# Every second attention head with V as the stationary operand, and VectorE's deferrable work emitted from one list

## The chip, the cores and the metric

The kernel runs on one core of a Trainium2 chip. Its time is the device time of that core in microseconds, the median of three runs. A profile of one further execution shows what each engine did: TensorE (PE, its weight loads apart as PEld), VectorE (DVE), ScalarE (ACT), GpSimd (POOL) and SyncE (SP), which here only starts transfers.

## What is computed

A layer norm of x (2048 tokens by 512), then two branches that are multiplied and added to x: attention over a cache of 2048 keys in 32 heads of 128, and a dense layer with a squared ReLU, through a SiLU. All tensors are bfloat16.

```python
xn = layernorm(x)                                    # 2048 x 512
q  = (xn @ wq).reshape(S, 32, 128)                   # per head
p  = softmax(q @ k_cache[h].T * 128**-0.5)           # 2048 x 2048 per head
s  = concat_h(p @ v_cache[h]) @ wo                   # 4096 -> 512
h  = relu(xn @ w1 + b1) ** 2                         # 512 -> 1792
g  = silu(h @ w2 + b2)                               # 1792 -> 512
out = x + s * g
```

## The kernel before

The kernel is one program in which every engine's instructions are laid out at build time, in order. It goes through 4 blocks of 512 queries x 32 heads = 128 "heads" g, each in 8 steps ("pairs" of key tiles): 1024 steps in all. In a step TensorE computes two score tiles (keys on the partitions, 512 queries along the row), ScalarE takes their exponential into one of 8 pT buffers, and TensorE multiplies pT of two steps ago with V. Between these lie the matmuls of the projections, of the dense branch and of the output projection, one or two per step, from a list of jobs; each job's result in one of two PSUM banks (psF) is taken out by VectorE.

The product of pT with V comes in two forms. In an ordinary head pT is the stationary operand, and V, with a column of ones for the softmax denominator, is streamed:

```python
# gen_pv: 8 matmuls of 129 columns in each of the 8 steps
t = E(PE, partial(_mm_shared, out=bankO(b)[:, qt % 2 * 256:qt % 2 * 256 + Dh + 1],
                  lhsT=pT[:, ps % NPT, p0:p0 + P],
                  rhs=v_sb[:, i, tt, 0:Dh + 1], ...))
# [...] at the end of the head: two copies out of PSUM, reciprocal, scaling, transposing DMA
```

In a V-stationary head V is the stationary operand and pT is streamed, so that the output comes transposed, as the output projection wants it, but without denominators. VectorE sums these from pT, and a trip through DRAM spreads them over the partitions:

```python
def is_b(g):
    return g % 4 == 1 and 4 < g < NG - 2           # 31 of the 128 heads

# gen_pv_b: 2 matmuls of 512 columns in each of the 8 steps
t_PV[pi] = E(PE, partial(_mm, out=bankO(0), lhsT=v_sb[:, i, tt, 0:Dh],
                         rhs=pT[:, pi % NPT, n * QB:(n + 1) * QB], ...))
# at the end of the head ScalarE copies the bank to o_b(g), a view of o_un

def den_part(pi):                                   # VectorE, once per step
    k = pi % NPR
    t_part[pi] = E(DV, partial(_reduce_t, out=d_part[:, k, :],
                               in_=pT[:, pi % NPT, :].rearrange("p (b j) -> p b j", j=32)),
                   deps=[t_exp[pi], t_den[0]])

def den_sum(g):                                     # d_sum, then DRAM and back
    t_den[0] = E(DV, partial(_reduce, out=d_sum[:], ...))
    t_den[1] = S.emit_dma(GP, partial(_dma, out=d_scr, in_=d_sum[:]), ...)
    for a in range(4):
        t_den[2] = S.emit_dma(GP, partial(_dma, out=d_quad[32 * a:32 * (a + 1), :, :], in_=src), ...)

def den_spread(g):                                  # d_rec: sum of 4, reciprocal; r_all: spread
    # [...]
def den_scale(g):                                   # oT = o_b(g) * r_all
    # [...]

def plan_b(g):                                      # fixed steps
    first = NPR * g + LAG
    for k in range(NPR):
        at_once.setdefault(first + 3 * k // 2, []).append(partial(den_part, NPR * g + k))
    at_once.setdefault(first + 12, []).append(partial(den_sum, g))
    at_once.setdefault(first + 19, []).append(partial(den_spread, g))
    at_once.setdefault(first + 20, []).append(partial(den_scale, g))
```

A pT buffer is written again 8 steps later, when both the matmuls and den_part have read it:

```python
t_exp[pi] = E(AC, partial(_act, out=pT[:, pi % NPT, :], in_=psA[...], func=ACT.Exp, ...),
              deps=[t, t_PV[pi - NPT] if pi >= NPT else None, t_part.get(pi - NPT)])
```

The two banks psO of an ordinary head are copied out by VectorE at its end (o_un); the next head's first product waits for the copy.

Of the kernel before, what the change touches and what calls it, by code (L numbers as in the profile page):

```python
# [227 lines left out]
def bass_recurrent_scan__mha_block_cached__dense_activation_squared_relu__prompt_kernel(  # L228
# [33 lines left out]
    LAG = 2  # L262
    VW = 136
# [7 lines left out]
    E = S.emit  # L271
# [16 lines left out]
    o_un = sb("o_un", [P, 2, TPB, Dh + 2], F32)  # L288
    rden = sb("rden", [P, 2, TPB], F32)
# [25 lines left out]
    tmp_t = sb("tmp_t", [P, 2, D], F32)  # L315
# [31 lines left out]

    def is_b(g):
        return g % 4 == 1 and 4 < g < NG - 2
# [207 lines left out]
    def gen_scores(pi):  # L557
        g, k = divmod(pi, NPR)
        s2, i = pi % 2, g % NSL
        assert t_kfill[g] is not None and t_evac[g] is not None  # L560
        t = None
        if g == 0:
            qt, b = divmod(pi, 2)
            for c in range(NKT // 2):
                t = E(PE, partial(_mm_shared, out=psA[:, s2 * 1024 + c * P:s2 * 1024 + (c + 1) * P],
                                  lhsT=kT[:, 0, (b * NKT // 2 + c) * P:(b * NKT // 2 + c + 1) * P],
                                  rhs=qt_sb[:, 0, qt * P:(qt + 1) * P], start=True, stop=True),
                      deps=[t_k0[b], t_q0[qt], t_exp[pi - 2] if pi >= 2 else t_b1[0]],
                      inc=(c == NKT // 2 - 1))
        else:  # L570
            for n in range(2):
                tt = 2 * k + n
                t = E(PE, partial(_mm, out=psA[:, s2 * 1024 + n * 512:s2 * 1024 + (n + 1) * 512],
                                  lhsT=kT[:, i, tt * P:(tt + 1) * P], rhs=qt_sb[:, g % NQS, :],
                                  start=True, stop=True),
                      deps=[t_exp[pi - 2] if pi >= 2 else None, t_kfill[g], t_evac[g],
                            t_bankF[0] if pi == 0 else None],
                      inc=(n == 1))
        if k == NPR - 1:
            t_S_last[g] = t  # L580
        t_exp[pi] = E(AC, partial(_act, out=pT[:, pi % NPT, :],
                                  in_=psA[:, s2 * 1024:(s2 + 1) * 1024],
                                  func=ACT.Exp, scale=SM_SCALE),
                      deps=[t, t_PV[pi - NPT] if pi >= NPT else None, t_part.get(pi - NPT)])
# [3 lines left out]
    t_obf = [None, None]  # L588
    t_part = {}
    t_den = [None] * 6  # L590
    later = []

    def gen_pv_b(pi):
        g, k = divmod(pi, NPR)
        i = g % NSL
        for n in range(2):
            tt = 2 * k + n
            t_PV[pi] = E(PE, partial(_mm, out=bankO(0), lhsT=v_sb[:, i, tt, 0:Dh],
                                     rhs=pT[:, pi % NPT, n * QB:(n + 1) * QB],
                                     start=(tt == 0), stop=(tt == NKT - 1)),  # L600
                         deps=[t_exp[pi], t_vfill[g], t_free[0]], inc=(n == 1))
        if k == NPR - 1:
            t_PV_last[g] = t_PV[pi]
            t_free[0] = E(AC, partial(_act, out=o_b(g), in_=bankO(0), func=ACT.Copy),
                          deps=[t_PV[pi], t_onorm[g - 2]])

    def o_b(g):
        return o_un[:, g % 2, :, :].rearrange("p t c -> p (t c)")[:, 0:QB]
# [7 lines left out]
    def den_sum(g):  # L616
        t_den[0] = E(DV, partial(_reduce, out=d_sum[:],
                                 in_=d_part[:].rearrange("p k (n b) -> p b (k n)", n=2)),
                     deps=[t_part[NPR * (g + 1) - 1], t_den[1]])
        t_den[1] = S.emit_dma(GP, partial(_dma, out=d_scr, in_=d_sum[:]), sl_dw,  # L620
                              deps=[t_den[0], t_den[2]])
        src = bass.AP(tensor=d_scr.tensor, offset=d_scr.offset,
                      ap=[[NBK, 32], [32 * NBK, 4], [1, NBK]])
        free = [t_den[1], t_den[3]]
        for a in range(4):
            t_den[2] = S.emit_dma(GP, partial(_dma, out=d_quad[32 * a:32 * (a + 1), :, :],
                                              in_=src), sl_dr, deps=free)

    def den_spread(g):
        t_den[3] = E(DV, partial(_reduce, out=d_rec[:],  # L630
                                 in_=d_quad[:].rearrange("p a b -> p b a")),
                     deps=[t_den[2], t_den[5]])
        t_den[4] = E(DV, partial(_recip, out=d_rec[:], in_=d_rec[:]), deps=[t_den[3]])
        base = d_rec[:]
# [5 lines left out]
    def den_scale(g):  # L640
        t_onorm[g] = tok_oT[g] = E(
# [3 lines left out]

    def plan_b(g):
        first = NPR * g + LAG
        for k in range(NPR):
            at_once.setdefault(first + 3 * k // 2, []).append(partial(den_part, NPR * g + k))
        at_once.setdefault(first + 12, []).append(partial(den_sum, g))  # L650
        at_once.setdefault(first + 19, []).append(partial(den_spread, g))
        at_once.setdefault(first + 20, []).append(partial(den_scale, g))

    def gen_pv(pi):
# [34 lines left out]
        if last:  # L689
            t_PV_last[g] = t  # L690
            s = g % 2
            for b in range(2):
# [3 lines left out]
                    deps=[t_bank[b], t_onorm[g - 2] if g >= 2 else None])  # L696
            tr = E(DV, partial(_recip, out=rden[:, s, :], in_=o_un[:, s, :, Dh]),
                   deps=[t_oev[g][0], t_oev[g][1], t_onorm[g - 2] if g >= 2 else None])
            base = rden[:, s, :]
            rb = bass.AP(tensor=base.tensor, offset=base.offset,  # L700
                         ap=[list(base.ap[0]), [1, TPB], [0, Dh]])
            t_onorm[g] = E(DV, partial(_tt, out=o_bf[:, s, :, :], in0=o_un[:, s, :, 0:Dh], in1=rb,
                                       op=ALU.mult),
                           deps=[tr, t_obf[s]])

    def gen_oT(g):
        if is_b(g):
            return
        tok_oT[g] = t_obf[g % 2] = S.emit_dma(
            SP, partial(_dmaT, out=oT[:, g % NOT, :].rearrange("p (t q) -> p t q", q=P),  # L710
                        in_=o_bf[:, g % 2, :, :].rearrange("p t d -> p (t d)")), sl_oT[g % 4],
# [5 lines left out]
    t_o2 = {}  # L717
    t_g = {}
    t_acc = {}
    t_u = {}  # L720
    t_outdma = [None, None]
# [6 lines left out]
    at_once = {}  # L728
# [27 lines left out]
    def job_h(j, c):  # L756
# [11 lines left out]
        def evac(bank, step):  # L768
            s = c % 2
            t1 = E(DV, partial(_ts, out=r_t[:, s, :], in0=bankF(bank), scalar1=b1f[:, c:c + 1],  # L770
                               scalar2=0.0, op0=ALU.add, op1=ALU.max),
                   deps=[box[0], t_b1[0], t_rt[s]])
            t_h2[j, c] = t_rt[s] = E(
                DV, partial(_tt, out=h2T[:, c, :], in0=r_t[:, s, :], in1=r_t[:, s, :],
                            op=ALU.mult),
                deps=[t1] + [t_o2[j - 1, qt] for qt in range(TPB) if j > 0])
# [3 lines left out]
    def job_o2(j, qt):  # L780
        jt = j * TPB + qt

        def mm(n, bank):
# [3 lines left out]
            if t is not None:  # L787
                t_o2[j, qt] = t

        def evac(bank, step):  # L790
            s = jt % 2
            tz = E(DV, partial(_tt, out=z_t[:, s, :], in0=bankF(bank), in1=b2bc[:], op=ALU.add),
                   deps=[t_o2[j, qt], tok_b2, t_zrd[s]])
# [13 lines left out]
            at(step + 3, gate)  # L807
# [5 lines left out]
    def job_wo(j, m, qt, c0=0, c1=D):  # L813
# [6 lines left out]
        def mm(n, bank):  # L820
            g = j * H + h0 + n
            place, free = (bankF(bank), t_bankF[bank]) if isinstance(bank, int) else bank
# [6 lines left out]
        def evac(bank, step):  # L829
# [11 lines left out]
            if m == len(CH[j]) - 2:  # L841
                at(step + 1, partial(pre_combine, j, qt))
            if last:
                s = jt % 2
                t = E(DV, partial(_stt, out=tmp_t[:, s, c0:c1], in0=place, scalar=0.5,
                                  in1=g_all[:, jt % (2 * TPB), c0:c1], op0=ALU.mult,
                                  op1=ALU.mult),
                      deps=[box[0], t_g[jt], t_tmp[s]])
# [21 lines left out]
    def pre_combine(j, qt):  # L870

        jt = j * TPB + qt
        if jt not in t_g:
            pending.append(partial(pre_combine, j, qt))
            return
        t = E(DV, partial(_stt, out=acc[:, qt, :], in0=acc[:, qt, :], scalar=0.5,
                          in1=g_all[:, jt % (2 * TPB), :], op0=ALU.mult, op1=ALU.mult),
              deps=[t_acc[qt], t_g[jt]])
        t_u[jt] = E(DV, partial(_tt, out=acc[:, qt, :], in0=acc[:, qt, :], in1=x_t[:, qt, :],
                                op=ALU.add), deps=[t, tok_xt[jt]])  # L880

# [4 lines left out]
    for j in range(NQB):  # L886
# [7 lines left out]
        for m, (h0, h1) in enumerate(CH[j]):  # L894
            if h1 == H and j == NQB - 1:
                continue
            for qt in range(TPB):
                r = j * SPB + NPR * h1 + (14 if h1 < H else 30)
                jobs.append((r + 30 + 15 * qt, r, job_wo(j, m, qt), None))
# [40 lines left out]
    def tail_one(step):  # L940
        i, x = tail_order[0]
        if step < NPAIR and step < NPR * ((NQB - 1) * H + CH[-1][-1][0] + x + 1) + 10:
            return False
# [60 lines left out]
    for j in range(NQB):  # L1004
        if j + 1 < NQB:
            for i in range(TPB):
                at(j * SPB + 3 * NPR, partial(ln_load, j + 1, i))
                at(j * SPB + 7 * NPR + 3 * i, partial(ln_stats, j + 1, i))
                at(j * SPB + 10 * NPR + 6 + NPR * i, partial(ln_next, j + 1, i))
# [65 lines left out]
    for pi in range(NPAIR):  # L1075
# [22 lines left out]
        for fn in at_once.pop(pi, []):  # L1098
            fn()
# [5 lines left out]
        if k == LAG + 1 and g >= 1:  # L1105
            gen_oT(g - 1)
        pending.extend(events.pop(pi, []))
        if k >= 2:
            for fn in [pending.pop(0) for _ in range(min(2, len(pending)))]:
                fn()  # L1110
    for pi in range(NPAIR - LAG, NPAIR):
        gen_pv(pi)
    gen_oT(NG - 1)
# [9 lines left out]
    assert not jobs and cur[0] is None and not events and not pending and not at_once  # L1123
# [32 lines left out]
```

## Time and profile before

| | |
|---|---|
| time, median of 3 runs | 1241.03 us (1239.99 to 1245.44) |
| span of the profiled execution | 1236.9 us |
| granted TensorE clock | 1.0 throughout |
| DMA, mean | 148 GB/s |

The page lists each engine's busy time, and groups of equal instructions as "out<-in" with their count, busy time and mean duration; behind it stands the idle time of the engine just before them and what ended it. Matmuls overlap, so their duration is longer than the distance from one start to the next. In the page's slices of the span ScalarE and VectorE look like this, in tenths of a fortieth:

```profile
DVE  4576655477766656546776666554686765556655
ACT  7888888888888888888888888888888888888894
```

The longest waits of the profile are VectorE's and GpSimd's, and are idle time of engines that have time to spare:

```profile
POOL d_scr L221 <- DVE d_sum L209: 892.8, 31, 60.0
DVE o_un L180 <- PE psO L158: 209.0, 85, 6.7
...
DVE d_rec L209 <- DMA d_quad<-d_scr: 46.4, 20, 6.0
```

The numbers behind the colon are microseconds in total, the number of waits, and the longest.

### The profile page before, as it was taken

To read this page: it belongs to the slowest core of one execution; us is meant where nothing else is said; L and a number is where in the kernel's file an instruction comes from. 1 tells how busy PE (TensorE), PEld (TensorE's weight loads), DVE (VectorE), ACT (ScalarE), POOL (GpSimd) and SP (SyncE) were. 2 spreads that over 40 slices of the span, in tenths; PEclk is the share of its full clock that TensorE was granted. 3 is DMA by queue.
4 is the path that set the end of the run, shared out by engine and by line. 5 is a ranking of instruction groups with operands and counts; after the bars stand their busy time and mean duration, and the time that the engine had idled before them with its cause. 6 is when DMAs were issued, how large, how long until landed. Compare 5 with 4: busy or idle time off the path is not lost.

```text
span 1236.9 us, 24563 instructions
## 1 busy us (share of the span) xinstructions
PE 1227.2 (99%) x10397; PEld 754.9 (61%) x10397; DVE 770.2 (62%) x1232; ACT 1062.6 (86%) x1075; POOL 117.7 (10%) x228
## 2 busy tenths in 40 slices
PE   9999999999999999999999999999999999999998
PEld 7665556655666655665555665556656556656565
DVE  4576655477766656546776666554686765556655
ACT  7888888888888888888888888888888888888894
POOL 1010100000012010000000201000000000100001
PEclk9999999999999999999999999999999999999999
DMA  9998987676788696877677878786777679787661
GB/s 219 213 222 168 192 193 130 135 139 132 137 156 153 121 173 137 147 141 131 130 132 170 149 133 159 141 150 130 136 146 135 139 151 147 147 142 143 133 121 28
DMA packets 674957, 182.47 MB, mean 148 GB/s; under 512 B 659152, under 2 KB 673664, under 8 KB 674848
## 3 DMA queue, kind: packets, MB, share of 16 engines
q1 hardware_dynamic: 667792, 175.55, 75.1%
q0 software_dynamic: 6384, 5.09, 2.3%
q8 instruction: 82, 1.34, 0.5%
q10 hardware_dynamic: 672, 0.26, 0.1%
q14 instruction: 27, 0.22, 0.1%
HBM read 97.62 MB, written 2.35 MB: 81 GB/s over the span
## 4 chain that ended last, share of the span: by engine, by line
PE 88%; DVE 6%; DMA 4%; issue 1%; POOL 1%; SPq 0%; DVEq 0%
PE psA L153 32%; PE psO L158 25%; PE psF L153 23%; PE psO L153 8%; DVE d_part L213 2%; DMA d_quad<-d_scr 2%; DMA d_scr<-d_sum 1%; POOL d_quad L221 1%; DVE qt_sb L180 0%; DVE r_t L172 0%; DVE acc L166 0%; DMA kT<-in_A_k_cache_dram 0%; DVE o_un L180 0%; DVE oT L166 0%; DVE h2T L166 0%
## 5 line engine op out<-in xcount | busy, mean ns | idle before, releaser
L162 ACT ACTIVATE pT<-psA 128x1024 bf16<-128x1024 f32 x1024 | 1040.9, 1024 | 153.9 <-PE psA L153 115.3
L153 PE MATMUL psA<-qt_sb,kT 128*128 128x512 bf16 x2032 | 604.3, 379 | 0.0
L158 PEld LDWEIGHTS psO<-v_sb,pT 128*128 128x128 bf16 x6208 | 414.7, 98 | 186.5 <-issue 13.1
L158 PE MATMUL psO<-v_sb,pT 128*128 128x129 bf16 x6208 | 478.2, 220 | 3.8 <-DVE o_un L180 3.8
L213 DVE TRANSPOSE_TENSOR_REDUCE d_part<-pT 128x32 f32<-128x1024 bf16 x248 | 291.9, 1217 | 0.0
L180 DVE COPY o_un<-psO 128x258 f32<-128x258 f32 x194 | 73.8, 421 | 209.6 <-PE psO L158 209.0
L153 PEld LDWEIGHTS psA<-qt_sb,kT 128*128 128x128 bf16 x2032 | 167.1, 98 | 58.6
L153 PE MATMUL psF<-xnT,wq_sb 128*128 128x512 bf16 (+1 forms) x520 | 168.7, 374 | 0.1
L153 PE MATMUL psF<-wo_all,oT 128*128 128x512 bf16 x480 | 163.7, 379 | 1.6 <-DVE oT L166 1.6
L153 PE MATMUL psO<-pT,v_sb 128*128 128x512 bf16 x496 | 147.5, 379 | 0.0
L180 DVE CAST qt_sb<-psF 128x512 bf16<-128x512 f32 (+1 forms) x130 | 86.6, 666 | 56.1 <-PE psF L153 55.7
L221 POOL DMA_DIRECT2D d_scr<-d_sum x31 | 17.4, 562 | 892.8 <-DVE d_sum L209 892.8
L153 PEld LDWEIGHTS psF<-xnT,wq_sb 128*128 128x128 bf16 x520 | 50.3, 98 | 59.8 <-DVE xnT L180 0.2
L153 PEld LDWEIGHTS psO<-pT,v_sb 128*128 128x128 bf16 x496 | 48.5, 98 | 58.6 <-issue 2.8
L153 PEld LDWEIGHTS psF<-wo_all,oT 128*128 128x128 bf16 x480 | 46.9, 98 | 58.3 <-DVE oT L166 2.1
L153 PE MATMUL psF<-xnT,w_sb 128*128 128x512 bf16 x224 | 77.1, 379 | 0.0
L153 PE MATMUL psF<-w_sb,h2T 128*128 128x512 bf16 x224 | 74.1, 379 | 0.0
L221 POOL DMA_DIRECT2D d_quad<-d_scr x124 | 67.6, 552 | 68.1 <-DMA d_scr<-d_sum 64.8
L166 DVE TENSOR_TENSOR o_bf<-o_un,rden 128x512 bf16<-128x512 f32 x97 | 67.1, 692 | 3.8 <-DVE rden L184 0.5
L172 DVE TENSOR_SCALAR r_t<-psF,b1f 128x512 bf16<-128x512 f32 x56 | 41.2, 736 | 45.2 <-PE psF L153 45.2
L153 PEld LDWEIGHTS psF<-w_sb,h2T 128*128 128x128 bf16 x224 | 21.9, 98 | 26.4
L153 PEld LDWEIGHTS psF<-xnT,w_sb 128*128 128x128 bf16 x224 | 21.9, 98 | 26.4
(58 smaller groups left out, 338.8 us busy)
## 6 DMA issues: line engine op xcount, KB each, us to landing
v_sb<-in_A_v_cache_dram SPq DMA_DIRECT2D x127, 512.0 KB, 4.6
wq_sb<-in_A_wq_dram SPq DMA_DIRECT2D x127, 128.0 KB, 3.3
wo_all<-in_A_wo_dram SPq DMA_DIRECT2D x4, 1024.0 KB, 6.1
w_sb<-in_B_w_dram SPq DMA_DIRECT2D x14, 256.0 KB, 4.3
x_t<-in_A_x_dram POOLq DMA_DIRECT2D x16, 128.0 KB, 3.4
kT<-in_A_k_cache_dram SPq DMA_TRANSPOSE x127, 4.4
d_quad<-d_scr POOLq DMA_DIRECT2D x124, 8.0 KB, 3.5
x_ln<-in_A_x_dram SPq DMA_DIRECT2D x15, 128.0 KB, 3.8
```

The lines of the kernel that those rows point to most:

```text
L153: return e.matmul(out, lhsT, rhs, start=start, stop=stop)
L158: return e.matmul(out, lhsT, rhs, start=start, stop=stop, skip_group_check=True)
L162: return e.activation(out, in_, func, bias=bias, scale=scale)
L166: return e.tensor_tensor(out, in0, in1, op)
L172: return e.tensor_scalar(out, in0, scalar1=scalar1, scalar2=scalar2, op0=op0, op1=op1)
L180: return e.tensor_copy(out, in_)
L213: return e.tensor_reduce(out, in_, axis=AX.X, op=ALU.add, apply_transpose=True)
L221: return e.dma_start(out, in_)
```

## The change

Three things. First, V is stationary in every second head from 4 to 124, 61 instead of 31. Second, VectorE's work that nobody waits for at once (the denominators' parts and their end, the normalising of ordinary heads, the squaring in the dense branch, gating, layer norm of the next block) is no longer put at fixed steps but into one list, each entry with the first step at which it may be emitted and the step at which it must. At build time an account is kept of how far TensorE and VectorE have come; a piece is emitted when VectorE is no more than ROOM = 1000 ns ahead of TensorE in this account (250 ns in the first step of a head), or when it is due. Third, V-stationary heads get output buffers of their own (o_col), and the buffers of the ordinary heads are counted by ordinary heads alone, so that each kind alternates between two; room for it comes from letting tmp_t be z_t.

```diff
+    clock = {"PE": 0.0, "DVE": 0.0}
+    def E(eng, fn, deps=(), inc=True):
+        if eng is PE:
+            clock["PE"] += free_size(fn.keywords["out"]) / 2.4 + 2.5
+        elif eng is DV:
+            n = max(free_size(fn.keywords[k]) for k in ("out", "in_") if k in fn.keywords)
+            clock["DVE"] = max(clock["DVE"], clock["PE"]) + n / 0.96 + 75
+        return S.emit(eng, fn, deps=deps, inc=inc)
[...]
+    o_col = sb("o_col", [P, 2, QB], F32)
-    tmp_t = sb("tmp_t", [P, 2, D], F32)
+    tmp_t = z_t
[...]
+    b_heads = [g for g in range(4, NG - 3, 2)]
     def is_b(g):
-        return g % 4 == 1 and 4 < g < NG - 2
+        return g in b_no
[...]
     def plan_b(g):
-        first = NPR * g + LAG
+        first = NPR * g
         for k in range(NPR):
-            at_once.setdefault(first + 3 * k // 2, []).append(partial(den_part, NPR * g + k))
-        at_once.setdefault(first + 12, []).append(partial(den_sum, g))
-        at_once.setdefault(first + 19, []).append(partial(den_spread, g))
-        at_once.setdefault(first + 20, []).append(partial(den_scale, g))
+            calm(first + k + 1, first + k + NPT - 2, partial(den_part, NPR * g + k))
+        calm(first + NPR, first + NPR + 8, partial(den_sum, g))
+    def fill_quiet(step, room, flush=False):
+        while quiet:
+            some = [x for x in quiet if may_run(x, step, flush)]
+            some = [x for x in some if x is not fresh[0]] or some
+            if not some:
+                break
+            x = min(some, key=lambda x: x[1])
+            if not flush and step < x[1] and clock["DVE"] - clock["PE"] > room:
+                break
+            fn = x[2].pop(0)
+            fn()
+            fresh[0] = x
+            if not x[2]:
+                quiet.remove(x)
+            if fn.func is den_sum:
+                g = fn.args[0]
+                calm(step + 10, step + 16, partial(den_total, g), partial(den_recip, g),
+                     partial(den_spread, g), partial(den_scale, g))
[...]
             for b in range(2):                        # end of an ordinary head
                 t_free[b] = t_oev[g][b] = E(DV, partial(_copy, out=o_un[...], in_=bankO(b)...), ...)
-            tr = E(DV, partial(_recip, ...))
-            t_onorm[g] = E(DV, partial(_tt, out=o_bf[:, s, :, :], ...))
+            calm(pi + LAG, pi + LAG + 3, partial(norm_recip, g), partial(norm_scale, g))
[...]
-            t_h2[j, c] = t_rt[s] = E(DV, partial(_tt, out=h2T[:, c, :], ...))
+            calm(step, step + 3, square)
-            at(step + 3, gate)
+            calm(step + 3, step + 8, gate)
-                at(step + 1, partial(pre_combine, j, qt))
+                calm(step + 1, step + 16, partial(acc_gate, j, qt), partial(acc_add, j, qt))
[...]
-                r = j * SPB + NPR * h1 + (14 if h1 < H else 30)
-                jobs.append((r + 30 + 15 * qt, r, job_wo(j, m, qt), None))
+                r = j * SPB + NPR * h1 + (24 if h1 < H else 30)
+                jobs.append((r + 20 + 15 * qt, r, job_wo(j, m, qt), None))
[...]
-                at(j * SPB + 7 * NPR + 3 * i, partial(ln_stats, j + 1, i))
-                at(j * SPB + 10 * NPR + 6 + NPR * i, partial(ln_next, j + 1, i))
+                b = j * SPB + 8 * NPR + 4 * NPR * i
+                calm(b, b + 24, partial(ln_bn, j + 1, i), partial(ln_rstd, j + 1, i))
+                calm(b + 28, b + 48, partial(ln_scale, j + 1, i), partial(ln_transpose, j + 1, i))
[...]
-        for fn in at_once.pop(pi, []):
-            fn()
+        fill_quiet(pi, 250 if k == 0 else ROOM)
```

The output projection of a group of heads is released 10 steps later, as a V-stationary head's output may now come later; its deadline stays. The matmuls of the last group are let in 26 steps after a V-stationary head's end instead of 10.

## The prediction

> **What bounds the kernel now.** I read four views in this order: the page's engine line, the costliest groups, the waits, and two stretches of the timeline.
>
> The engine line and two groups of the page:
>
> ```profile
> span 1236.9 us, 24563 instructions
> PE 1227.2 (99%) x10397; PEld 754.9 (61%) x10397; DVE 770.2 (62%) x1232; ACT 1062.6 (86%) x1075; POOL 117.7 (10%) x228
> ...
> L158 PE MATMUL psO<-v_sb,pT 128*128 128x129 bf16 x6208 | 478.2, 220 | 3.8 <-DVE o_un L180 3.8
> L213 DVE TRANSPOSE_TENSOR_REDUCE d_part<-pT 128x32 f32<-128x1024 bf16 x248 | 291.9, 1217 | 0.0
> ...
> L153 PE MATMUL psO<-pT,v_sb 128*128 128x512 bf16 x496 | 147.5, 379 | 0.0
> ```
>
> TensorE is busy for 99% of the span, VectorE for 62%, ScalarE for 86%. The mean of a matmul (220 or 379 ns) is its latency, not its price: matmuls overlap, so the price has to come from starts. The chain of waits gives it:
>
> ```profile
> 1221.64 1.36 PE psO L158 x24
> 1223.00 3.45 PE psF L153 x16
> ```
>
> A 129-column matmul takes 1.36/24 = 0.0567 us of TensorE, a 512-column one 3.45/16 = 0.2156 us. That these two prices explain the whole span shows that TensorE is the bound: 6208 x 0.0567 = 352 us, and (2032 + 504 + 480 + 496 + 224 + 224 + 16, all 512 wide by their groups) 3976 x 0.2156 = 857 us, together 1209 us. The small matmuls of start and end add about 15 us. What is left, some 12 us, is the wait for the first data, the drain at the end and stalls.
>
> How much of it is stall is in the waits of TensorE:
>
> ```profile
> PE psO L158 <- DVE o_un L180: 3.8, 5, 1.5
> PE psF L153 <- DVE oT L166: 1.6, 1, 1.6
> ```
>
> Six stalls, 5.4 us. As a matmul's shown end lies 0.16 us behind the next one's start, each is 0.16 us longer than shown: 6.4 us. The timeline shows how one comes about, VectorE first and TensorE below it:
>
> ```profile
> 273.62 0.26 DVE L209 TENSOR_REDUCE d_rec<-d_quad 128x16 f32<-128x64 f32 x1 [3.33 <-DMA d_quad<-d_scr]
> ...
> 276.73 0.68 DVE L166 TENSOR_TENSOR oT<-o_un,r_all 128x512 bf16<-128x512 f32 x1
> 277.51 0.76 DVE L180 COPY o_un<-psO 128x258 f32<-128x258 f32 x2
> ```
> ```profile
> 276.43 0.38 PE L153 MATMUL psF<-wo_all,oT 128*128 128x512 bf16 x1
> 278.09 0.53 PE L158 MATMUL psO<-v_sb,pT 128*128 128x129 bf16 x6 [1.28 <-DVE o_un L180]
> ```
>
> VectorE stood 3.33 us in front of d_rec until the softmax denominators came back from DRAM. Behind it in the queue stood gating, a projection cast, the scaling, and only then the copy that frees the output bank. TensorE needed that bank at 276.65 and had it at 278.09.
>
> [...]the copy above waits behind a DMA that it doesn't need, and 98 ns of weight load per matmul don't show in a pitch of 56.7 ns. [...]six transpose-reductions in 6.79 us, 1.13 us each for 1024 elements[...].
>
> **The change part by part.**
>
> *30 more heads with V stationary (31 to 61).* An ordinary head has 64 matmuls of 129 columns, 64 x 0.0567 = 3.63 us; a V-stationary one has 16 of 512, 16 x 0.2156 = 3.45 us. That is 0.18 us a head, and x 30 it is 5.3 us, on the engine that sets the end. The gain comes only from the ones column (one in 129) and the fixed share per matmul: the product itself is as large as before.
>
> *What VectorE pays.* Such a head needs 8 transpose-reductions (8 x 1.13 = 9.04), d_sum 0.58, d_rec 0.26 + 0.25, r_all 0.71 and oT 0.69: 11.5 us. It saves two output copies (0.84), a reciprocal (0.18) and o_bf (0.69): 1.7 us. Net 9.8 us, x 30 = 295 us. VectorE goes from 770 to about 1065 us, 86% of a span near 1230. This is off the path as long as its order is right.
>
> *Where it is tightest.* A pair of heads takes 2 x 1236.9/128 = 19.3 us now. VectorE needs 11.5 + 1.7 for it, and a share of the rest: 770.2 - 31 x 11.5 - 97 x 1.7 = 249 us over 64 pairs, 3.9 us. Sum 17.1, 89%. Following the new order of instructions from one d_sum to the next in a stretch with the output projection (3 copies or adds of partial sums, 2 gatings, 2 casts, beside the two heads' own), the mean durations add to some 18.7 us; neighbours overlap by about 0.08 us (1.217 against 1.13), so some 17 us of 19.1. I find no stretch whose work is above TensorE's, so no stall is forced by quantity. Moments are left.
>
> *The deferred list.* It takes nothing away from VectorE; it moves the d_part, normalising, squaring, gating and layer-norm instructions so that they are emitted when VectorE is less than 1.0 us ahead of TensorE by the account, 0.25 us at a head's first step, just before the bank copies. The account's costs (1024/0.96 + 75 = 1142 ns for a d_part, 608 for 512 elements) are near the trace's pitch of 1130. And d_rec is now emitted at least 10 steps after d_sum, 10 x 1.2 = 12 us, where it was 7 steps, 8.4 us. The trip in the chain takes 3.38 (write) + about 0.3 + 1.62 (issue) + 3.85 (read) = 9.2 us. So the kind of wait shown above should nearly vanish. Of the 6.4 us of stalls I count 5 as removed, the one before the tail (oT of head 125) among them, as the last V-stationary head is now 124.
>
> *The rest.* ScalarE: 30 more copies of an output bank x 0.592 = 18 us, to 1080 us, still below 90%. GpSimd: 5 issues x 0.55 us x 30 = 83 us, at 16% nobody waits for it. 30 transposing DMAs of oT fall away. The separate o_col buffers let V-stationary outputs wait for scaling without holding the ordinary heads' copies. The z_t buffer now serves tmp_t as well, which ties the gating to the final combination; with few of them in a stage it should cost nothing.
>
> *Sum.* -5.3 - 5 + new stalls. For these I take 4 us: about one in four of the 60 changes to a V-stationary head meets a d_part of 1.13 us just begun and loses about 0.25 us. Net -6.3, 1241.0 to 1234.7; rounded to 1234.
>
> **The rivals.**
>
> *A: VectorE becomes the bound in moments.* It holds 1.1-us instructions, with 2 us to spare in two heads, and a late d_part holds its pT buffer, then the exponential eight pairs on, then TensorE. For it: the load near 90%, and the account that puts tiny instructions at 75 to 80 ns where d_sum alone takes 580. Against it: exponentials have about 0.2 us per pair in hand (1.02 against 1.2) and scores run two pairs ahead. It would cost 5 to 20 us and make 1236 to 1250.
>
> *B: The DRAM trip comes late more often.* 61 trips, one every 19 us; the longest read in the chain took 5.12 us, 1.3 more than usual, and d_sum itself can run a microsecond or two after its emission. If one trip in four blocks VectorE as at 273 us, at 1.4 us each, that is 21 us: 1250. Against it: of the 20 times VectorE waited for this DMA (46 us) only a few reached TensorE, even with 3.6 us less room.
>
> *C: All old stalls vanish and no new ones come.* 1241.0 - 5.3 - 6.4 = 1229.3. For it speaks that the account is fitted to the trace's pitch; against it, that 60 changes of head must then all go well.
>
> **Range and chances.** C is the floor, as nothing else on TensorE is removed; a mild form of A makes the upper end. 1229 to 1242 should hold it 8 times in 10. Over 2% faster would be under 1216, below the floor: 0.01. Over 2% slower, above 1266, needs A and B together or a dependence that I overlook: 0.03. Within 2%: 0.96.
>
> **What would show it right or wrong.** Right: 67 x 64 = 4288 matmuls psO<-v_sb,pT instead of 6208 and 61 x 16 = 976 psO<-pT,v_sb instead of 496, TensorE still at 99%, VectorE at 86%, idle time before d_rec below 46 us in spite of twice as many, TensorE's waits for o_un and oT at a few us in all. Wrong: waits of TensorE for o_un, of ScalarE for d_part, or of psF matmuls for a cast, adding up to more than 10 us; or VectorE idle in front of d_rec as before. A pitch other than 0.0567 and 0.2156 us[...] would break the first term.

## The result, and the profile after

The changed kernel takes 1229.63 us (median of 4 runs, 1229.31 to 1231.01) against 1241.48 us for the kernel before in the same comparison: a ratio of 0.9902, 95% interval 0.9877 to 0.9926. That is 1.0% less, inside the predicted range and at its fast end.

The page of the changed kernel, the engine line and the groups that answer to those shown before:

```profile
span 1229.2 us, 22035 instructions
PE 1213.5 (99%) x8793; PEld 694.7 (57%) x8957; DVE 1028.9 (84%) x1502; ACT 1071.3 (87%) x1105; POOL 200.5 (16%) x378
...
L213 DVE TRANSPOSE_TENSOR_REDUCE d_part<-pT 128x32 f32<-128x1024 bf16 x488 | 575.4, 1216 | 0.0
...
L158 PE MATMUL psO<-v_sb,pT 128*128 128x129 bf16 x4288 | 330.2, 220 | 0.8 <-ACT pT L162 0.3
L153 PE MATMUL psO<-pT,v_sb 128*128 128x512 bf16 x957 | 286.2, 379 | 0.8
```

VectorE works 259 us more (a d_part takes 1216 ns on the mean, 1217 before) and TensorE is still busy throughout. 164 matmul records are missing in this trace (8793 matmuls, 8957 weight loads), which is why 957 stand where 976 ran; a gap of one matmul's length in it is no stall. The pitch has not changed. In the chain of waits of this kernel:

```profile
1190.13 0.68 PE psO L158 x12
...
1216.83 1.29 PE psA L153 x6
```

0.68/12 = 0.0567 us and 1.29/6 = 0.215 us, as before.

What changed most is the list of waits. These are VectorE's in front of d_rec and all three of TensorE's:

```profile
DVE d_rec L209 <- DMA d_quad<-d_scr: 2.7, 1, 2.7
...
PE psA L153 <- POOL mhalf L188: 1.0, 1, 1.0
PE psO L197 <- DMA kT<-in_A_k_cache_dram: 0.7, 1, 0.7
PE psO L158 <- ACT pT L162: 0.3, 1, 0.3
```

The first two of TensorE's lie in the first 6 us, the last behind the last exponential; in between the view lists none. Both waits shown before (for o_un and for oT) are gone, and VectorE stands in front of d_rec for 2.7 us instead of 46.4, with twice as many trips.

To see where the time went, I cut each trace at two instructions that all versions share, the start of the 9th and of the last exponential. Most experiments are read in these stretches too.

| us | up to 9th exponential | 9th to last (1015 steps) | last to end | span |
|---|---|---|---|---|
| before | 17.06 | 1202.65 | 17.17 | 1236.9 |
| after | 18.70 | 1192.53 | 17.98 | 1229.2 |
| 31 heads with the list (experiment 1) | 17.18 | 1197.73 | 16.02 | 1230.9 |

The middle gained 10.1 us. The first stretch lasted 1.6 us longer in this one execution. Some 0.9 us of it is the first K tile, which came later (its first use starts at 5.72 us instead of 4.79); in nearly the same program, experiment 3, the stretch took 17.03. This execution (1231.01 us) is also the slowest of the four, so the median carries little of it. The end, which should have gained too, lost 0.8 us.

### The profile page after: what moved, and what is told of

Same layout as the page of the kernel before. It is cut to its first block, busy times and chain, and to the rows that moved or that the text cites. A ratio compares the mean times of both kernels' runs of the same rounds, so it can differ in the third digit from the quotient of the medians.

```text
span 1229.2 us, 22035 instructions
## 1 busy us (share of the span) xinstructions
PE 1213.5 (99%) x8793; PEld 694.7 (57%) x8957; DVE 1028.9 (84%) x1502; ACT 1071.3 (87%) x1105; POOL 200.5 (16%) x378
## 3 DMA queue, kind: packets, MB, share of 16 engines
q0 software_dynamic: 11184, 6.32, 3.0%
## 4 chain that ended last, share of the span: by engine, by line
PE 98%; issue 1%; DMA 0%; ACT 0%; DVE 0%; ACTq 0%; SPq 0%; DVEq 0%
PE psA L153 35%; PE psF L153 25%; PE psO L158 20%; PE psO L153 17%; DMA kT<-in_A_k_cache_dram 0%; ACT pT L162 0%; PE psA L158 0%; PE psO L197 0%; PE psF L197 0%; DVE out_t L166 0%; DVE z_t L176 0%; ACTq L135 0%; DVE xnT L180 0%; SPq L221 0%; PE psA L197 0%
## 5 line engine op out<-in xcount | busy, mean ns | idle before, releaser
L153 PE MATMUL psA<-qt_sb,kT 128*128 128x512 bf16 x1909 | 577.8, 379 | 5.8
L213 DVE TRANSPOSE_TENSOR_REDUCE d_part<-pT 128x32 f32<-128x1024 bf16 x488 | 575.4, 1216 | 0.0
L158 PEld LDWEIGHTS psO<-v_sb,pT 128*128 128x128 bf16 x4288 | 286.6, 98 | 125.2 <-ACT pT L162 0.6
L158 PE MATMUL psO<-v_sb,pT 128*128 128x129 bf16 x4288 | 330.2, 220 | 0.8 <-ACT pT L162 0.3
L153 PE MATMUL psO<-pT,v_sb 128*128 128x512 bf16 x957 | 286.2, 379 | 0.8
L153 PEld LDWEIGHTS psO<-pT,v_sb 128*128 128x128 bf16 x976 | 95.4, 98 | 115.2 <-issue 5.8
L221 POOL DMA_DIRECT2D d_quad<-d_scr x244 | 132.9, 551 | 144.6 <-DMA d_scr<-d_sum 139.3
L180 DVE COPY o_un<-psO 128x258 f32<-128x258 f32 x134 | 51.0, 422 | 124.2 <-PE psO L158 123.7
L166 DVE TENSOR_TENSOR oT<-o_col,r_all 128x512 bf16<-128x512 f32 x61 | 41.9, 687 | 2.6
L217 DVE STREAM_TRANSPOSE r_all<-d_rec 128x512 f32<-128x512 f32 x61 | 43.1, 707 | 1.2
```

Source lines behind the costliest of these rows:

```text
L153: return e.matmul(out, lhsT, rhs, start=start, stop=stop)
L158: return e.matmul(out, lhsT, rhs, start=start, stop=stop, skip_group_check=True)
L166: return e.tensor_tensor(out, in0, in1, op)
L180: return e.tensor_copy(out, in_)
L213: return e.tensor_reduce(out, in_, axis=AX.X, op=ALU.add, apply_transpose=True)
L217: return e.transpose(out, in_)
```

## The experiments

Theory: two separate gains, cheaper products in 30 more heads and fewer stalls through the order of VectorE's work. Rivals: only one of the two counts; or VectorE is at its edge; or only one feature of the new order (the later reading of the denominators, the buffers, the gate at a head's start) does it all.

### 1. The list with 31 heads

```diff
-    b_heads = [g for g in range(4, NG - 3, 2)]
+    b_heads = [g for g in range(4, NG - 3, 4)]
```

> The changed kernel with only 31 V-stationary heads (every fourth, 4 to 124) and all else as it is. Theory (two separate sources: wider matmuls 5.3 us, stalls removed by the list about 5 us): 1229.6 + 30 x 0.177 = 1234.9 us, 1233.5 to 1236.5, with TensorE's waits under 2 us. Rival 'the list alone' (the wider matmuls bring nothing that lasts): 1229 to 1231. Rival 'the wider matmuls alone': near the kernel before, 1239 to 1242.

Measured: 1232.79 us (1232.71 to 1232.88), ratio to before 0.9926 (0.9914 to 0.9939). Both sources exist, but the time missed my window. In the middle stretch the list (with its buffers and the later reading of the denominators) gives 1202.65 - 1197.73 = 4.92 us, and the 30 heads another 1197.73 - 1192.53 = 5.20, or 0.173 us a head, as worked out. The 2.0 us that the sum then lacks are in the last column: 16.02 us with 31 heads, 17.98 with 61.

### 2. 61 heads with the fixed steps

```diff
-        return g % 4 == 1 and 4 < g < NG - 2
+        return g % 2 == 0 and 3 < g < NG - 3
```

(and the last group's matmuls let in 18 steps after a V-stationary head's end instead of 10; the change takes 26.)

> The kernel before, with its fixed steps, and 61 V-stationary heads (every second, 4 to 124). Theory: 5.3 us less matmul time, but twice as many trips that VectorE waits for in front of work that TensorE needs, so stalls of 12 to 25 us in place of 6: 1241.5 - 5.3 + 6 to 19 = 1242 to 1255 us. Rival 'the wider matmuls alone': 1229 to 1236, as VectorE's 84% leaves room in any order. VectorE's idle time in front of d_rec: 70 us or more by the theory.

Measured: 1302.21 us (ratio 1.0493, 1.0473 to 1.0513). I had the direction and not the size: it is 60 us above the kernel before in the same comparison (1241.93). The waits of this kernel, TensorE's first:

```profile
PE psA L153 <- ACT pT L162: 14.1, 32, 1.2
PE psF L153 <- DVE r_t L172: 9.9, 10, 2.3
PE psF L153 <- DVE z_t L166: 9.8, 6, 3.2
PE psO L158 <- ACT o_un L162: 7.4, 9, 2.0
```
```profile
DVE d_rec L209 <- DMA d_quad<-d_scr: 111.6, 55, 5.4
...
ACT pT L162 <- DVE d_part L213: 37.9, 53, 2.2
```

VectorE loses 112 us in front of d_rec at a load of 81%; what it then does late holds up everybody: exponentials that wait for a pT buffer, psF banks, and the output bank through ScalarE's copy into the shared o_un.

### 3 and 4. No gate at the head's start; no account at all

```diff
-        fill_quiet(pi, 250 if k == 0 else ROOM)
+        fill_quiet(pi, ROOM)      # experiment 3
+        fill_quiet(pi, 1e9)       # experiment 4
```

> The changed kernel with the lead of 1000 ns allowed at every step, also at a head's first one (250 ns there in the change). Theory (the order at the change of heads matters): a d_part of 1.13 us stands in front of the bank copies o_un more often, TensorE waits for o_un 2 to 10 us in all: 1231 to 1239. Rival (the slack of a head is enough by itself): 1229 to 1231, waits for o_un under 1 us.

Measured: 1229.96 us (ratio 0.9905, 0.9890 to 0.9921), the middle stretch 1192.88 against 1192.53. No wait of TensorE for o_un at all. The gate is worth nothing that can be seen; the rival holds.

> The changed kernel without the account: each piece is emitted in the first step in which it is allowed, soonest deadline first. Theory (the account is what keeps VectorE's queue short in front of bank copies): d_part pieces come in bunches behind the d_rec chain and TensorE waits 8 to 40 us for o_un and psF banks: 1237 to 1270. Rival (later reading of the DRAM trip is all that counted): 1229 to 1232.

Measured: 1341.02 us (ratio 1.0812, 1.0789 to 1.0835), beyond my window. The same work, in another order. Of TensorE's waits 80.7 us are for results to be taken out of psF, these two groups the longest; for o_un it waits once, 0.3 us, so that half of the theory was wrong:

```profile
PE psF L153 <- DVE r_t L172: 24.4, 25, 3.6
PE psF L153 <- DVE acc L166: 21.6, 16, 2.6
```

Its timeline, VectorE first, then TensorE:

```profile
305.54 0.76 DVE L180 COPY o_un<-psO 128x258 f32<-128x258 f32 x2 [4.35 <-PE psO L158]
...
315.98 4.60 DVE L213 TRANSPOSE_TENSOR_REDUCE d_part<-pT 128x32 f32<-128x1024 bf16 x4
320.62 0.58 DVE L209 TENSOR_REDUCE d_sum<-d_part 128x16 f32<-128x256 f32 x1
321.11 0.69 DVE L166 TENSOR_TENSOR acc<-psF,acc 128x512 f32<-128x512 f32 x1
```
```profile
321.86 0.39 PE L153 MATMUL psF<-wo_all,oT 128*128 128x512 bf16 x1 [1.36 <-DVE acc L166]
```

VectorE idles 4.35 us before a head's end, has four d_part pieces and a d_sum in a row ten microseconds later, and TensorE's bank is emptied behind them. Here deadlines alone were not enough; the work had to be spread.

### 5. A lead of 3000 ns

```diff
-        fill_quiet(pi, 250 if k == 0 else ROOM)
+        fill_quiet(pi, 3000)
```

> The changed kernel with VectorE allowed to be 3000 ns ahead of TensorE in the account at every step (1000 in e3: 1230 us; without limit in e4: 1341 us). Theory: a psF bank is filled about every 3.4 us and must be empty by the time of the job after next, so a lead of 3 us plus the copy is just too much: 1235 to 1270 us, waits of TensorE for psF results. Rival (only a lead without limit hurts): 1229 to 1232.

Measured: 1246.40 us (ratio 1.0049, 1.0035 to 1.0062); middle stretch 1209.34, so 16.5 us more than with 1000 at every step (experiment 3). The time is in the window, but the reason I gave, psF banks, is only part of it: 5.2 us of TensorE's waits are for exponentials, against 5.2 us for results out of psF.

```profile
PE psA L153 <- ACT pT L162: 5.2, 7, 0.9
PE psF L153 <- DVE z_t L166: 2.0, 4, 0.6
PE psF L153 <- DVE r_t L172: 1.5, 2, 1.2
PE psF L153 <- DVE acc L166: 1.1, 3, 0.4
...
PE psF L153 <- DVE z_t L176: 0.6, 1, 0.6
```

### 6. The denominators read 7 steps after their sum

```diff
-                calm(step + 10, step + 16, partial(den_total, g), partial(den_recip, g),
+                calm(step + 7, step + 7, partial(den_total, g), partial(den_recip, g),
                      partial(den_spread, g), partial(den_scale, g))
```

> The changed kernel with the end of the denominators (d_rec and on) put 7 steps after d_sum, due at once, instead of 10 to 16. Theory (a queue in order waits for the DRAM trip of about 9 us, 7 steps are 8.4): VectorE idle in front of d_rec 40 to 150 us in all instead of 2.7, time 1233 to 1260. Rival (the later reading is not what helped): 1229 to 1231.

Measured: 1247.06 us (ratio 1.0051, 1.0035 to 1.0066). This kernel's waits:

```profile
DVE d_rec L209 <- DMA d_quad<-d_scr: 50.2, 29, 3.4
...
PE psA L153 <- ACT pT L162: 6.5, 12, 1.7
```

Both numbers lie in the theory's windows, and the kind of cost is the one that rival B of the prediction feared. The edit does two things, though: the end of the denominators comes three steps earlier, and it is due at once, so that the account can no longer put it off. How much of the 17 us the second one costs was not tested; the 50.2 us in front of d_rec show the first.

### 7. Is the later reading enough at fixed steps?

With 31 heads, in the kernel before:

```diff
-        at_once.setdefault(first + 19, []).append(partial(den_spread, g))
-        at_once.setdefault(first + 20, []).append(partial(den_scale, g))
+        at_once.setdefault(first + (22 if g < NG - 3 else 19), []).append(partial(den_spread, g))
+        at_once.setdefault(first + (23 if g < NG - 3 else 20), []).append(partial(den_scale, g))
```

> The kernel before, 31 V-stationary heads at fixed steps, with one thing moved: the end of the denominators (d_rec and on) 10 steps after d_sum instead of 7 (head 125 keeps its steps). If the list's gain at 31 heads (4.9 us between the ninth and the last exponential) is only the later reading: the same stretch 1197.7 to 1198.5 us instead of 1202.65, time about 1236. If the account is needed too: 1200 to 1203, time 1238 to 1241. VectorE idle in front of d_rec below 10 us either way.

In this kernel the copy of head g+2 and the scaling of head g fall into one step, the copy first and into the same o_un buffer, so the scaling multiplies what the copy has put there; the amount of work is the same. Measured: 1238.41 us (ratio 0.9987, 0.9980 to 0.9994), middle stretch 1202.28. VectorE's idle time in front of d_rec fell from 46 to 14 us (I had said below 10), and little came of it: 1.6 us of the time, 0.4 of the middle stretch. Its waits, and VectorE's order in front of one of them (TensorE goes on at 316.18):

```profile
PE psO L158 <- DVE o_un L180: 2.8, 6, 0.5
PE psF L153 <- DVE oT L166: 1.3, 1, 1.3
```
```profile
313.30 0.75 DVE L172 TENSOR_SCALAR r_t<-psF,b1f 128x512 bf16<-128x512 f32 x1 [2.31 <-PE psF L153]
314.09 0.42 DVE L166 TENSOR_TENSOR h2T<-r_t 128x512 bf16<-128x512 bf16 x1
314.43 0.26 DVE L209 TENSOR_REDUCE d_rec<-d_quad 128x16 f32<-128x64 f32 x1
314.72 0.25 DVE L184 RECIPROCAL d_rec<-d_rec 128x16 f32<-128x16 f32 x1
315.01 0.71 DVE L217 STREAM_TRANSPOSE r_all<-d_rec 128x512 f32<-128x512 f32 x1
315.64 0.72 DVE L180 COPY o_un<-psO 128x258 f32<-128x258 f32 x2
```

Six shorter waits for o_un stand where five longer ones were. In all six the denominators' end, which no longer waits for its transfer, stands right in front of the copy. Moving it to this fixed step moved the collision; whether another fixed step would avoid it was not tested.

With 61 heads, own buffers o_col for the V-stationary heads and the later reading, or with the buffers alone (in both tmp_t is z_t, and the last group's matmuls are let in after 26 steps, as in the change; the ordinary heads' buffers are not counted anew):

```diff
     def o_b(g):
-        return o_un[:, g % 2, :, :].rearrange("p t c -> p (t c)")[:, 0:QB]
+        return o_col[:, g // 2 % 2, :]
[...]
-        at_once.setdefault(first + 19, []).append(partial(den_spread, g))   # second kernel only
-        at_once.setdefault(first + 20, []).append(partial(den_scale, g))
+        at_once.setdefault(first + 22, []).append(partial(den_spread, g))
+        at_once.setdefault(first + 23, []).append(partial(den_scale, g))
```

> As e11 (61 V-stationary heads at fixed steps, separate output buffers, 1242 us), but with d_rec read 7 steps after d_sum as in the kernel before. e2, without the separate buffers, took 1302 us. If the buffers alone make the 60 us between e2 and e11: 1242 to 1247. If the early reading makes most of it: 1275 to 1300, with VectorE idle in front of d_rec near e2's 112 us. From the early reading's cost under the list (17 us in e6) I expect 1255 to 1270.

> 61 V-stationary heads at fixed steps as in e2 (1302 us), with the change's separate output buffers for them and the later reading, without list and account. If buffers and reading are what e2 lacked: 1229 to 1236 us. If the account is the main part: 1255 to 1295, with TensorE waiting for psF banks behind d_part pieces, and ScalarE for d_part.

Measured: 1299.29 us with the buffers alone (ratio 1.0493, 1.0459 to 1.0528), 1241.86 with both (1.0013, 1.0006 to 1.0019). For the buffers alone, the window of the early reading held and my own guess between the two did not; neither of the two windows of the second kernel was right. From experiment 2 to the change the way is now: 1302.2, buffers 1299.3, later reading 1241.9, all the rest 1229.6: 3, 57 and 12 us. The 3 us of the buffers are no more than differences between comparisons: both ratios are 1.0493. The reading is the large part, but only at fixed steps (at most 17 us under the list, experiment 6). The 12 us are the list with its account, together with the ordinary heads' own count of buffers and the later release of the output projection, which no run separates; without them the kernel would not have been faster than before. VectorE's idle time in front of d_rec with the buffers alone, then the waits with both, d_rec's among them:

```profile
DVE d_rec L209 <- DMA d_quad<-d_scr: 105.3, 54, 7.4
```
```profile
ACT pT L162 <- DVE d_part L213: 23.9, 32, 2.0
...
DVE d_rec L209 <- DMA d_quad<-d_scr: 8.3, 7, 2.9
...
PE psA L153 <- ACT pT L162: 6.3, 9, 1.9
```

### 8. How much room VectorE has

An idle reduction of pT, its result unused, in front of the den_part of one or two steps of every V-stationary head, unknown to the account:

```diff
     def den_part(pi):
         k = pi % NPR
+        if k in (0,):                                  # second kernel: (0, 4)
+            t_idle[0] = S.emit(DV, partial(_reduce_t, out=d_idle[:],
+                in_=pT[:, pi % NPT, :].rearrange("p (b j) -> p b j", j=32)),
+                deps=[t_exp[pi], t_idle[0]])
```

> The changed kernel with one idle transpose-reduction (1.13 us, its result unused) more in each of the 61 V-stationary heads, unknown to the account, so that all else keeps its order. VectorE 1029 + 61 x 1.13 = 1098 us, 89%. Theory (VectorE costs nothing until the work of two heads passes TensorE's 19.1 us; 16.1 + 1.1 = 17.2): 1229 to 1233 us. Rival (VectorE is already at the edge in moments): 1238 or more.

> The same with two idle reductions per V-stationary head: 1029 + 122 x 1.13 = 1167 us, 95%; two heads 18.4 us on the mean, above 19.1 in the stretches with the output projection. Theory: time starts to rise, 1233 to 1255 us, with TensorE waiting for psF banks. Rival (only the whole sum counts, and it is still below TensorE's): 1229 to 1232.

Measured: 1231.84 us (ratio 0.9933, 0.9916 to 0.9950) and 1254.49 us (1.0117, 1.0102 to 1.0132). Their engine lines:

```profile
PE 1222.0 (99%) x8957; PEld 693.3 (56%) x8957; DVE 1093.3 (89%) x1563; ACT 1071.6 (87%) x1105; POOL 200.6 (16%) x378
```
```profile
PE 1227.1 (98%) x8957; PEld 690.3 (55%) x8957; DVE 1159.3 (92%) x1624; ACT 1070.6 (85%) x1105; POOL 200.5 (16%) x378
```

The first 64 us of VectorE work cost 2.2 us, the next 66 cost 22.7 (the middle stretch: 1192.53 in the change, 1194.64, 1217.46). So the changed kernel, at 84%, stands below a steep rise and not at it. This holds for work that the account does not know of; with such work planned in, the rise may come later, which was not tested. In the second kernel TensorE waits 9.3 us for results to be taken out of psF, as I had said, and as long, 8.9 us, for the copies at a head's end, for which no other kernel with the list made it wait more than 0.3 us:

```profile
PE psO L153 <- DVE o_un L180: 8.9, 13, 1.3
PE psF L153 <- DVE r_t L172: 6.3, 7, 1.0
```

### 9. The end of the span

What ends last in the changed kernel is neither a transfer nor a result, but GpSimd's closing drain, the instruction DRAIN at the end of its program (start at 1222.3 us, beside GpSimd's last addition of 1.3 us; 6705 ns, so to 1229.0; SyncE's last wait was over at 1226.8). From the views of that source line, the end of the program's block, for before, the change and the 31-head version of experiment 1:

```profile
L135 POOLq DRAIN  x1: 4660/4660/4660, 1231.9 to 1231.9; - x1
```
```profile
L135 POOLq DRAIN  x1: 6705/6705/6705, 1222.3 to 1222.3; - x1
...
L135 SPq DRAIN  x1: 7/7/7, 1227.0 to 1227.0; - x1
L135 SPq EVENT_SEMAPHORE  x1: 17/17/17, 1229.2 to 1229.2; - x1
```
```profile
L135 POOLq DRAIN  x1: 4253/4253/4253, 1226.0 to 1226.0; - x1
```

In the change SyncE is done at 1227.0 and its closing semaphore comes only at 1229.2, behind GpSimd's; in the other two GpSimd's drain is over 0.1 and 0.5 us before SyncE's begins and costs nothing. GpSimd had started 185, 335 and 185 transfers. To take transfers away, the sums are written to DRAM in an order that one transfer can read:

```diff
-        t_den[1] = S.emit_dma(GP, partial(_dma, out=d_scr, in_=d_sum[:]), sl_dw, ...)
+        dst = bass.AP(tensor=d_scr.tensor, offset=d_scr.offset,
+                      ap=[[NBK, 4], [4 * NBK, 32], [1, NBK]])
+        t_den[1] = S.emit_dma(GP, partial(_dma, out=dst, in_=d_sum[:]), sl_dw, ...)
         src = bass.AP(tensor=d_scr.tensor, offset=d_scr.offset,
-                      ap=[[NBK, 32], [32 * NBK, 4], [1, NBK]])
-        for a in range(4):
-            t_den[2] = S.emit_dma(GP, partial(_dma, out=d_quad[32 * a:32 * (a + 1), :, :], in_=src), ...)
+                      ap=[[0, 4], [4 * NBK, 32], [1, 4 * NBK]])
+        t_den[2] = S.emit_dma(GP, partial(_dma, out=d_quad[:].rearrange("p a b -> p (a b)"), in_=src), ...)
```

> The changed kernel with the denominators' trip in 2 transfers instead of 5: d_sum is written to DRAM in another order, so that one transfer reads all of d_quad. GpSimd starts 152 transfers instead of 335. Theory (GpSimd's closing drain, which ends the span of the 61-head kernels, grows with the number of transfers it has started: 4.3 to 4.7 us at 185, 6.3 to 6.7 at 335): drain about 4 us, SyncE's last wait ends the span instead, 2 us less: 1227 to 1228.5 us. Rival (the drain follows the bytes or the work in the tail): drain 6 us or more, 1229 to 1231.

Measured: 1227.70 us (1227.37 to 1227.79), ratio to before 0.9900 (0.9885 to 0.9914), and 1.9 us below the change. The two ratios, 0.9900 and 0.9902, do not separate the kernels, as the kernel before took 1240.06 us in this comparison and 1241.48 in the other; the traces do. The middle stretch is the same 1192.53 us; the stretch from the last exponential to the end is 16.00 us instead of 17.98. Its drain:

```profile
L135 POOLq DRAIN  x1: 3760/3760/3760, 1221.0 to 1221.0; - x1
```

The rival that bytes set it falls: this kernel moved 6.50 MB on GpSimd's queue, the change 6.32. Between transfers and packets the change doesn't decide, as both fell (335 to 152, and 11184 to 6304), but experiment 1 speaks for transfers: against its 185 transfers and 6384 packets this kernel has nearly the same packets, and a drain shorter by 0.49 us. From 185 to 335 it grew by 2.45 us, 16 ns a transfer, and 33 fewer transfers at that price make 0.54. Equal counts differ by up to 0.4 us between kernels, though, so this stays an estimate.

## Why the prediction was right

*The product term* (5.3 us) was measured as 5.2, and the prices behind it (0.0567 and 0.2156 us a matmul) held. Split into a share per column and a fixed one per matmul, they give 0.415 ns and about 3 ns, an estimate from these two prices alone. By this estimate the 48 matmuls fewer make 0.15 of the 0.18 us that a V-stationary head saves, and the ones column the rest.

*The stalls removed* (5 of 6.4 us) were in fact nearly all: 4.9 us in the middle, and the wait for oT before the tail. SyncE's last wait is over 16.7 us after the last exponential in the kernel before, 15.6 us after the change, 1.1 less. That is rival C.

*The new stalls* (4 us, one change of heads in four losing 0.25 us) are the term that failed: there are none. I had taken it that a d_part just begun would often be in the way, and that the gate of 250 ns only lessened this. Experiment 3 shows that not even the gate is needed at this load, and experiment 8 that such waits begin two reductions per head later. Most of the distance from the central value to the measured time comes from this term. (The sum itself gave 1234.7, which I rounded to 1234.)

*Rival A* did not come. I had put the load at 89% of a pair of heads; 84% of the span was measured, and the steep rise lies between 89% and 92%. Among its reasons I wrote that the account puts d_sum at 75 to 80 ns; by the code it is 256/0.96 + 75 = 342 ns, against 579 in the trace.

*What I had not in the sum* is the end: about +2 us of GpSimd's drain. I wrote that at 16% nobody waits for GpSimd; for TensorE that is right between the first 6 us, in which it waited 1.0 us for it, and the last instruction.

*VectorE's load* came out at 1029 instead of 1065 us. Added up record by record, VectorE's work rose by 304 us, near the 295 that I had worked out; its busy time rose by only 259. Neighbouring records overlap: by 46 us in all in the kernel before, by 91 us after the change, where more of them stand behind each other. I had allowed for that in the d_part (1.13 us each) and nowhere else.

*Rival B* was the danger that the change met by design: experiments 2, 6 and 7 show what the DRAM trip costs when it is read too early, 57 us at fixed steps and up to 17 under the list.

The sum by the trace: -5.2 - 4.9 - 1.1 + 1.9 = -9.3 us, with the start of the run left out. The medians differ by 11.9 us; the interval of the ratio, worked on 1241.5, is 9.2 to 15.3, so the two agree at its edge. The 2.6 us between them lie in the spread of the kernel before: its profiled execution took 1238.68 us, 2.8 below the median of this comparison, and in later ones its median was between 1239.92 and 1241.93. That the measured time stands so near rival C's 1229.3 is therefore partly luck: the drain that C did not have took back about 2 us, and the kernel before happened to come out high.

## What to carry to other kernels

VectorE did what stood behind a wait only after it: in the kernel before, at 273 us, 3.33 us in front of d_rec held up a copy that did not need that transfer, and TensorE lost 1.28 us in front of the copy's bank. So put the reader of a long round trip a step or two beyond the measured trip (here 12 us where it took about 9), and then spread deferrable work by an account of both engines' time. Moving one item by hand to another fixed step only moved the collision in experiment 7. Before trusting an engine's free share, add idle work to it and look for the rise; here it came between 89% and 92%, for work that was not planned in. And look at what ends the span: of the 10.1 us gained in the middle, GpSimd's closing drain gave back about 2.

## What the runs showed of the hardware

GpSimd's closing drain took 3.76 us after 152 transfers (experiment 9), 4.25 and 4.66 after 185 (experiment 1 and the kernel before), and 6.7 (6695 to 6705 ns) after 335 (the change, experiment 6 and both kernels of experiment 8). In experiment 4, also with 335, it took about 6.3, an estimate: the span ends 6.48 us after GpSimd's last addition starts, and in the change the drain starts with that addition and ends some 0.2 us before the span. In the four traces with 335 it was the last to end, and the other engines' closing semaphores came behind it; in the three with 185 or 152 SyncE was later. SyncE's own drain took 7 ns in all seven. I had not expected either how much VectorE's order is worth: the same instructions took 1230 us in one order (VectorE at 84%) and 1341 us in another, where the same busy time would be 76% of the profiled 1345.7 us, an estimate.
